# Bucketed attention and a squared-relu layer on one core: two stages instead of a mix, weight rounding spread out

## The chip, the cores and the metric

The kernel runs on one core of a Trainium2 chip. Its time is the device time of one execution in microseconds, the median of several runs. The profile is of one more execution. TensorE (PE, its weight loads PEld), VectorE (DVE), ScalarE (ACT) and GpSimd (POOL) run their own instruction streams in order and wait for each other by semaphores; SyncE (SP) only issues transfers here.

## What is computed

```python
# q, k, v: (4 batches, 8 heads, 768, 64) f32; proj: (64, 6); w_in: (512, 2048), w_out: (2048, 512), both float64
q_bucket = bits(q @ proj > 0);  k_bucket = bits(k @ proj > 0)
scores = where(q_bucket == k_bucket, q @ k.T / 8, -1e9)
attn = exp(scores - max);  attn = attn / (attn.sum(-1) + 1e-9)
x = (attn @ v), heads side by side        # (3072 tokens, 512)
out = maximum(x @ w_in, 0)**2 @ w_out     # (3072, 512)
```

## The kernel before

Attention works on 16 pairs of heads (`pr`), four pairs to a batch, and on 6 key tiles of 128 (`kt`) for each pair: 96 steps `u`. Keys lie on partitions, the 768 queries on columns in two halves of 384 (`HS`).

- `load_pair` (L206) brings q, k and v of a pair, on SP's queue, two pairs ahead.
- `features` (L223) transposes a half of q or k with three TensorE transposes; ScalarE copies the result out (`feat`). `hash_bits` (L237) multiplies it with the projections, and VectorE turns the sign into bits.
- `score` (L269) adds a bf16 product of bits, which drives keys of other buckets far down, and the f32 product of features. Two heads lie on the two halves of the rows. ScalarE's exponentials (L285) go to a ring of 8 tiles. The two score tiles take four of the eight PSUM banks, so a score begins only when the exponentials of the step before have read them.
- `add_up` (L293) adds the exponentials on VectorE, one step later; `attend` (L303) multiplies them with v into `xo`, two steps later. `xo` has one buffer.
- `sum_up` (L320) sums over partitions with a matrix of ones in two blocks of 64 columns, adds a small number by a bf16 matmul, and transposes (`flip`). `normalize` (L334) takes one reciprocal, transposes it back (`recs`) and multiplies it into `x_t` of the batch.
- A general path (`general`, L491) recomputes all if the values are large; `peak` (L250) collects the largest |q| and |k| for that decision, which is made at the very end (L469 to L484).

The weights arrive as float64 and are rounded by hand in 32 pieces of 128 x 512: `load_weight` (GpSimd's queue), `part_weight` (VectorE L120 and L124, GpSimd L129 and L132, ScalarE L135 `one`) and `round_weight` (VectorE L145 and L149, GpSimd L152).

The second part, `hidden` (L360) and `project` (L373), works on a half batch of 384 tokens: 16 groups of 4 matmuls with relu (ScalarE) and square (VectorE), then 3 groups of 16 matmuls for the output. An f32 matmul is two TensorE instructions ("passes" below), so the profile counts twice as many. A hidden or output group uses one of two PSUM banks (`bank`), which features, hashes and sums use too.

The order of every engine is written out by hand. A step u issues: loads of a later pair, `score(u)`, two pieces of weights (as long as there are any, so in the first 17 steps), two preparations for the next pair (features, hashes, peaks: they fill the first five steps of a pair), `add_up(u-1)`, `attend(u-2)`, after the last key tile the sums and the product, and then some of the waiting second part (`fill`, L400), which exists from the end of the first batch, step 25, on. The rest of the second part runs after the last step.

Of the kernel before, what the change touches and what calls it, by code (L numbers as in the profile page):

```python
# [23 lines left out]
TINY = 2.0**-100  # L24
# [9 lines left out]
def kernel(  # L34
# [28 lines left out]

    glob = ctx.enter_context(tc.tile_pool(name="glob", bufs=1))
# [8 lines left out]
    const = fast.enter_context(tc.tile_pool(name="const", bufs=1))  # L73
    p_qk = fast.enter_context(tc.tile_pool(name="p_qk", bufs=2))
    p_v = fast.enter_context(tc.tile_pool(name="p_v", bufs=3))
    p_f = fast.enter_context(tc.tile_pool(name="p_f", bufs=2))
    p_x = fast.enter_context(tc.tile_pool(name="p_x", bufs=2))
    p_n = fast.enter_context(tc.tile_pool(name="p_n", bufs=1))
    p_r = fast.enter_context(tc.tile_pool(name="p_r", bufs=2))
    ps_s = fast.enter_context(tc.tile_pool(name="ps_s", bufs=2, space=PSUM))  # L80
    ps_o = fast.enter_context(tc.tile_pool(name="ps_o", bufs=1, space=PSUM))
    ps_1 = fast.enter_context(tc.tile_pool(name="ps_1", bufs=2, space=PSUM))
# [17 lines left out]
    def load_weight(i, pool):  # L100
        src, r, c, dst = pieces[i]
        if src.dtype != U64:
            nc.gpsimd.dma_start(out=dst, in_=src[r:r + P, c:c + PIECE])
# [8 lines left out]
    def part_weight(i, pool):  # L112
# [4 lines left out]
        power = pool.tile([P, PIECE], U32, name="power")  # L117
        top = pool.tile([P, PIECE], U32, name="top")
        one = pool.tile([P, PIECE], FP32, name="one")
# [48 lines left out]
    ones = const.tile([P, D], FP32, name="ones")  # L168
    tinies = const.tile([P, D], BF16, name="tinies")
    units = const.tile([P, HS], BF16, name="units")  # L170
    peaks = const.tile([P, 2, NP], FP32, name="peaks")
# [3 lines left out]
    def constants():  # L175
        N = NBITS
        for h in range(2):
            r = h * D
            nc.scalar.dma_start(out=pj[r:r + D], in_=proj)
# [16 lines left out]
        nc.vector.memset(tinies, SB * TINY)  # L196
        nc.vector.memset(units, 1.0)
# [8 lines left out]
    def load_pair(pr):  # L206
        b, j = divmod(pr, PB)
        tiles = []
        for src, pool, name in ((q, p_qk, "q_nat"), (k, p_qk, "k_nat"), (v, p_v, "v_nat")):
            pair = src[b, 2 * j:2 * j + 2]  # L210
            if src is v:
                t = pool.tile([P, 2, SB * D], FP32, name=name)
                nc.sync.dma_start(out=t, in_=pair.rearrange("h (p t) d -> p h (t d)", t=SB))
            else:
                t = pool.tile([P, SB, 2, D], FP32, name=name)
                for h in range(2):
                    nc.sync.dma_start(
                        out=t[:, :, h], in_=pair[h].rearrange("(p t) d -> p t d", t=SB)
                    )
# [30 lines left out]
    def peak(pr, w):  # L250
        nc.vector.tensor_reduce(
            out=peaks[:, w, pr:pr + 1], in_=nat[pr][w].rearrange("p t h d -> p (t h d)"),
            axis=AXL.X, op=ALU.max, apply_absolute_value=True,
        )

    def prepare(pr):
        for w in range(2):
            for r in range(2):
                yield features, (pr, w, r)
        for w in range(2):  # L260
            for r in range(2):
                yield hash_bits, (pr, w, r)
        for w in range(2):
            yield peak, (pr, w)
# [26 lines left out]
    totals, outs = {}, {}  # L291
# [25 lines left out]
    x_t = {}  # L317
    flips = {}

    def sum_up(pr, c):  # L320

        tot = bank("tot")
        for h in range(2):
            rows = tot[h * D:(h + 1) * D, 0:HS]
            nc.tensor.matmul(  # L325
                out=rows, lhsT=ones, rhs=totals[pr, h][:, c * HS:(c + 1) * HS],
                start=True, stop=False,
            )
            nc.tensor.matmul(out=rows, lhsT=tinies, rhs=units, start=False, stop=True)  # L329
        if c == 0:  # L330
            flips[pr] = p_n.tile([P, S], FP32, name="flip")
        nc.vector.transpose(out=flips[pr][:, c * HS:(c + 1) * HS], in_=tot[:, 0:HS])  # L332

    def normalize(pr):  # L334

        b, j = divmod(pr, PB)
        if j == 0:
            x_t[b] = p_x.tile([P, NFT, S], FP32, name="x_t")
        rec = p_n.tile([P, S // 32], FP32, name="rec")
        nc.vector.reciprocal(  # L340
            out=rec, in_=flips[pr].rearrange("p (n f) -> p n f", f=32)[:, :, 0]
        )
        recs = p_n.tile([P, S], FP32, name="recs")
        nc.vector.transpose(
            out=recs.rearrange("p (n f) -> p n f", f=32),
            in_=rec.rearrange("p (n o) -> p n o", o=1).to_broadcast([P, S // 32, 32]),
        )
        xo = outs.pop(pr)
        for c in range(2):
            cut = slice(c * HS, (c + 1) * HS)  # L350
            nc.vector.scalar_tensor_tensor(  # L351
                out=x_t[b][:, j, cut], in0=xo[:, c, 0:HS], scalar=xo[:, 1, HS:HS + 1],
                in1=recs[:, cut], op0=ALU.add, op1=ALU.mult,
            )

    gates = {}

    def hidden(b, c, ff, pool):  # L360
        hp = bank("hid")
        for ft in range(NFT):
            nc.tensor.matmul(  # L363
                out=hp[:, 0:HS], lhsT=w_in[:, ft, ff * P:(ff + 1) * P],
                rhs=x_t[b][:, ft, c * HS:(c + 1) * HS], start=(ft == 0), stop=(ft == NFT - 1),
            )
        r = p_r.tile([P, HS], FP32, name="r")
        nc.scalar.activation(out=r, in_=hp[:, 0:HS], func=ACTF.Relu)  # L368
        g = pool.tile([P, HS], FP32, name="gate")
        nc.vector.tensor_tensor(out=g, in0=r, in1=r, op=ALU.mult)  # L370
        gates[b, c, ff] = g

    def project(b, t):  # L373
        c, i = divmod(t, SB // 2)
        y = bank("y")
        for ff in range(NFF):
            nc.tensor.matmul(  # L377
                out=y, lhsT=gates[b, c, ff][:, i * P:(i + 1) * P], rhs=w_out[:, ff],
                start=(ff == 0), stop=(ff == NFF - 1),
            )  # L380
        o = p_r.tile([P, DM], FP32, name="o")
        nc.scalar.copy(out=o, in_=y)  # L382
        nc.sync.dma_start(out=out_v[b, t], in_=o)

    def mlp(b, pool):
        for c in range(2):
            for ff in range(NFF):
                yield 2.7, hidden, (b, c, ff, pool)
            for i in range(SB // 2):
                yield 14.2, project, (b, c * (SB // 2) + i)  # L390

    steps = [(pr, kt) for pr in range(NP) for kt in range(SB)]
    SHARE = 7.2
    AHEAD = 2
    todo = []
    credit = [0.0]

    def fill(n):  # L400
        credit[0] += n
        while todo and credit[0] > 0:
            cost, f, args = todo.pop(0)
            f(*args)
            credit[0] -= cost
        if not todo:
            credit[0] = min(credit[0], 0.0)

    with tc.manual_schedule():
        load_pair(0)  # L410
        make_identity(nc, ident)
        constants()
        for pr in range(1, AHEAD):
            load_pair(pr)
        for f, args in prepare(0):
            f(*args)

        late = ExitStack()
        early = ExitStack()
        p_w = early.enter_context(tc.tile_pool(name="p_w", bufs=3))  # L420
        p_g = None
        LEAD = 3
        moved = 0
        for i in range(LEAD):
            load_weight(i, p_w)

        prep = []
        for u in range(len(steps) + 4):
            if u < len(steps):
                pr, kt = steps[u]  # L430
                if kt == 0:
                    if pr + AHEAD < NP:
                        load_pair(pr + AHEAD)
                    if pr + 1 < NP:
                        prep = list(prepare(pr + 1))
                score(pr, kt)
            for _ in range(2):
                if moved <= len(pieces):
                    if moved + LEAD < len(pieces):
                        load_weight(moved + LEAD, p_w)  # L440
                    if moved < len(pieces):
                        part_weight(moved, p_w)
                    if moved >= 1:
                        round_weight(moved - 1)
                    moved += 1
            if p_g is None and moved > len(pieces):
                early.close()
                p_g = late.enter_context(tc.tile_pool(name="p_g", bufs=NFF + 2))
            for _ in range(2):
                if prep:  # L450
                    f, args = prep.pop(0)
                    f(*args)
            if 1 <= u <= len(steps):
                add_up(*steps[u - 1])
            if 2 <= u <= len(steps) + 1:
                attend(*steps[u - 2])
            if u >= 2:
                pr, kt = steps[min(u - 2, len(steps) - 1)]
                if kt == SB - 1 and u - 2 < len(steps):
# [218 lines left out]
```

## Time and profile before

| what | value |
|---|---|
| median of 3 runs | 1202.77 us (1201.63 to 1202.92) |
| profiled execution: time, span | 1201.52 us, 1199.8 us |
| busy: PE, DVE, ACT, POOL | 1107.1, 440.3, 266.5, 113.0 us |
| mean granted TensorE clock | 0.962 of 2.4 GHz |
| HBM read, written | 35.65 MB, 6.29 MB |

The span is the time from the first to the last instruction of the profile; what lies outside it is the difference to the execution's time. Busy times are unions on an engine. The mean hides stages: the first 25 steps are attention alone with the weights beside it for 17 of them, then the second part of a finished batch is mixed into the steps of the next, and the last batch's second part stands alone at the end. Each of these is read by itself below.

### The profile page before, as it was taken

What the parts mean: (1) busy time and instruction counts of PE and PEld (TensorE: products, weight loads), DVE (VectorE), ACT (ScalarE), POOL (GpSimd) and SP (SyncE); (2) the same over time, 40 slices, a digit from 0 to 9 for tenths busy, and PEclk for the clock granted to TensorE, in tenths of its full rate; (3) what the DMA queues carried; (4) which work ended last, traced back from release to release, by engine and by line L of the source; (5) the groups of instructions that cost most, each with busy time, mean ns of one, the idle gap of its engine ahead of it and who ended that gap; (6) DMA issues with size and microseconds to landing.
All of it is one profiled execution on the core that took longest, in us unless ns stands there. A gap on an engine that the chain in (4) does not pass through costs nothing.

```text
span 1199.8 us, 10401 instructions
## 1 busy us (share of the span) xinstructions
PE 1107.1 (92%) x4226; PEld 529.5 (44%) x4226; DVE 440.3 (37%) x645; ACT 266.5 (22%) x441; POOL 113.0 (9%) x136
## 2 busy tenths in 40 slices
PE   4646369999999999999999999999999999999997
PEld 2222124455445544455445544455445544554543
DVE  3788889442224322342124322342124321310200
ACT  2222234322122211322122311322122211110110
POOL 2666661000000000000000000000000000000000
PEclk9767769999999999999999999999999999999999
DMA  7343321110010100110010100110000000000000
GB/s 205 106 114 119 114 101 40 41 27 14 17 36 14 27 22 10 49 27 14 18 36 14 27 22 10 49 27 14 18 9 1 1 9 9 9 1 17 9 9 20
DMA packets 62806, 42.68 MB, mean 36 GB/s; under 512 B 51488, under 2 KB 55584, under 8 KB 62752
## 3 DMA queue, kind: packets, MB, share of 16 engines
q1 hardware_dynamic: 57984, 25.17, 8.1%
q0 software_dynamic: 4608, 16.78, 4.2%
q8 instruction: 35, 0.57, 0.2%
q14 instruction: 19, 0.16, 0.0%
q10 hardware_dynamic: 160, 0.00, 0.0%
HBM read 35.65 MB, written 6.29 MB: 35 GB/s over the span
## 4 chain that ended last, share of the span: by engine, by line
PE 83%; DVE 9%; issue 3%; POOL 3%; DMA 1%; ACT 0%; SPq 0%; POOLq 0%; DVEq 0%; ACTq 0%
PE y L377 28%; PE hid L363 28%; PE st L278 12%; PE xo L310 10%; PE hp L242 3%; PE tp L230 2%; DVE one L149 2%; DVE total L299 2%; DVE power L145 2%; PE tot L325 2%; DVE power L120 1%; POOL power L129 1%; DMA q_nat<-in_q_dram 1%; POOL power L132 1%; POOL raw L106 1%
## 5 line engine op out<-in xcount | busy, mean ns | idle before, releaser
L363 PE MATMUL hid<-x_t,w_in 128*128 128x384 f32 x1024 | 342.1, 490 | 2.4 <-DVE x_t L351 2.4
L377 PE MATMUL y<-w_out,gate 128*128 128x512 f32 x768 | 334.4, 594 | 0.0
L363 PEld LDWEIGHTS hid<-x_t,w_in 128*128 128x128 f32 x1024 | 190.9, 190 | 152.1 <-ACT e L285 7.8
L377 PEld LDWEIGHTS y<-w_out,gate 128*128 128x128 f32 x768 | 144.7, 190 | 184.0 <-issue 175.3
L370 DVE TENSOR_TENSOR gate<-r 128x384 f32<-128x384 f32 x128 | 71.5, 558 | 329.6 <-ACT r L368 329.6
L285 ACT ACTIVATE e<-st 128x768 f32<-128x768 f32 x192 | 145.2, 809 | 140.2 <-PE st L278 136.5
L278 PE MATMUL st<-feat,feat 64*128 64x384 f32 x768 | 163.8, 499 | 0.0
L299 DVE TENSOR_TENSOR total<-total,e 128x768 f32<-128x768 f32 x128 | 118.2, 970 | 99.1 <-ACT e L285 99.1
L310 PE MATMUL xo<-e,v_nat 128*64 128x384 f32 (+1 forms) x768 | 152.5, 521 | 1.7 <-issue 1.6
L368 ACT ACTIVATE r<-hid 128x384 f32<-128x384 f32 x128 | 62.7, 490 | 328.1 <-PE hid L363 328.1
L278 PE MATMUL st<-bits,bits 64*128 64x384 bf16 x384 | 71.6, 336 | 27.0 <-ACT e L285 26.8
L382 ACT COPY o<-y 128x512 f32<-128x512 f32 x24 | 14.0, 585 | 341.7 <-PE y L377 244.7
L310 PEld LDWEIGHTS xo<-e,v_nat 128*64 128x64 f32 x768 | 48.6, 141 | 82.9 <-issue 79.3
L278 PEld LDWEIGHTS st<-feat,feat 64*128 64x128 f32 x768 | 72.0, 195 | 27.4 <-issue 26.5
L278 PEld LDWEIGHTS <-bits 64*128 64x128 bf16 x384 | 20.4, 94 | 96.5 <-issue 81.7
L332 DVE STREAM_TRANSPOSE flip<-tot 128x384 f32<-128x384 f32 x32 | 18.4, 579 | 103.3 <-PE tot L329 103.3
L145 DVE SCALAR_TENSOR_TENSOR power<-raw,power 128x512 uint32<-128x512 uint32 x32 | 44.5, 1390 | 27.7 <-POOL power L132 27.7
L245 DVE TENSOR_SCALAR bits<-hp,bar_k,gain_k 128x384 bf16<-128x384 f32 x32 | 21.0, 675 | 87.6 <-PE hp L242 87.6
L135 ACT ACTIVATE one<-top 128x512 f32<-128x512 uint32 x32 | 20.0, 630 | 104.3 <-DVE top L124 104.3
L245 DVE TENSOR_SCALAR bits<-hp,bar_q,gain_q 128x384 bf16<-128x384 f32 x32 | 20.7, 673 | 60.8 <-PE hp L242 60.8
L242 PE MATMUL hp<-feat,proj_k 128*128 128x384 f32 x64 | 29.0, 582 | 14.7 <-DVE bits L245 14.7
L325 PE MATMUL tot<-total,ones 128*64 128x384 f32 x128 | 28.6, 529 | 11.8 <-ACT feat L235 11.8
(55 smaller groups left out, 436.5 us busy)
## 6 DMA issues: line engine op xcount, KB each, us to landing
raw<-in_moe_w_in_dram POOLq DMA_DIRECT2D x16, 512.0 KB, 4.3
raw<-in_moe_w_out_dram POOLq DMA_DIRECT2D x16, 512.0 KB, 3.6
q_nat<-in_q_dram SPq DMA_DIRECT2D x32, 192.0 KB, 3.7
k_nat<-in_k_dram SPq DMA_DIRECT2D x32, 192.0 KB, 4.0
v_nat<-in_v_dram SPq DMA_DIRECT2D x16, 384.0 KB, 3.3
out_dram<-o SPq DMA_DIRECT2D x24, 256.0 KB, 2.0
pj<-in_proj_dram ACTq DMA_DIRECT2D x2, 1.5 KB, 2.3
```

Of the source, the lines that this page charges most:

```text
L145: nc.vector.scalar_tensor_tensor(out=power, in0=high, scalar=0x80000000, in1=power, op0=ALU.bitwise_and, op1=ALU.bitwise_or,)
L242: nc.tensor.matmul(out=hp[:, 0:HS], lhsT=projs[w], rhs=feat[pr, w][:, cut], start=True, stop=True)
L245: nc.vector.tensor_scalar(out=bits[pr, w][:, cut], in0=hp[:, 0:HS], scalar1=bars[w], scalar2=gains[w], op0=ALU.is_gt, op1=ALU.mult,)
L278: nc.tensor.matmul(out=st[h][:, c, 0:HS], lhsT=src[pr, 1][rows, key], rhs=src[pr, 0][rows, cut], start=first, stop=not first,)
L285: nc.scalar.activation(out=e[:, 0:S].rearrange("p (c f) -> p c f", c=2), in_=st[h][:, :, 0:HS], func=ACTF.Exp, scale=scale,)
L299: nc.vector.tensor_tensor(out=totals[pr, h], in0=in0, in1=weights[pr, kt, h][:, 0:S], op=ALU.add)
L310: nc.tensor.matmul(out=xo[h * D:(h + 1) * D, c, 0:n], lhsT=nat[pr][2][:, h, kt * D:(kt + 1) * D], rhs=weights[pr, kt, h][:, c * HS:c * HS ...
L325: nc.tensor.matmul(out=rows, lhsT=ones, rhs=totals[pr, h][:, c * HS:(c + 1) * HS], start=True, stop=False,)
L363: nc.tensor.matmul(out=hp[:, 0:HS], lhsT=w_in[:, ft, ff * P:(ff + 1) * P], rhs=x_t[b][:, ft, c * HS:(c + 1) * HS], start=(ft == 0), stop=( ...
L368: nc.scalar.activation(out=r, in_=hp[:, 0:HS], func=ACTF.Relu)
L370: nc.vector.tensor_tensor(out=g, in0=r, in1=r, op=ALU.mult)
L377: nc.tensor.matmul(out=y, lhsT=gates[b, c, ff][:, i * P:(i + 1) * P], rhs=w_out[:, ff], start=(ff == 0), stop=(ff == NFF - 1),)
```

## The change

- Two stages. The attention stage writes all of its output into one tile `x_t` of 4 x 3072 columns in SBUF; the second part follows in a stage of its own, with its own pools: 4 PSUM banks for hidden groups, 4 for outputs, 32 gate buffers.
- The second part works on 6 chunks of 512 tokens instead of 8 of 384.
- A piece of weights is loaded (on SP's queue, two raw buffers), parted and rounded in every third step, so all 96 steps have weights.
- `PREPARE` spreads the preparation of the next pair over all six steps.
- `sum_up` comes ahead of `attend` in its step. It sums in four column blocks of 32 (half and head), one f32 matmul each, and VectorE adds the small number (`once`), takes eight reciprocals of 32 partitions x 12, which also sort the blocks, and transposes back once.
- The largest |q| and |k| are collected in the second stage, from q and k loaded again in 16 pieces of 768 KB; the decision (`guard`) is made in chunk 3.
- The first k comes by ScalarE's queue, `proj` by GpSimd's.

```diff
-    p_x = fast.enter_context(tc.tile_pool(name="p_x", bufs=2))
+    x_t = fast.enter_context(tc.tile_pool(name="x_all", bufs=1)).tile([P, NFT, B * S], FP32, name="x_t")
+    p_w = first.enter_context(tc.tile_pool(name="p_w", bufs=2))
-        raw = pool.tile([P, PIECE, 2], U32, name="raw", bufs=4)
-        nc.gpsimd.dma_start(
+        raw = p_w.tile([P, PIECE, 2], U32, name="raw")
+        nc.sync.dma_start(
...
+        one = p_w.tile([P, PIECE], FP32, name="one")
+        top = one.bitcast(U32)
...
+    PREPARE = (
+        ((features, 0, 0), (features, 0, 1)),
+        ((features, 1, 0),),
+        ((features, 1, 1), (hash_bits, 0, 0)),
+        ((hash_bits, 0, 1),),
+        ((hash_bits, 1, 0),),
+        ((hash_bits, 1, 1),),
+    )
...
-    def sum_up(pr, c):
+    def sum_up(pr):
         tot = bank("tot")
-        for h in range(2):
-            rows = tot[h * D:(h + 1) * D, 0:HS]
-            nc.tensor.matmul(
-                out=rows, lhsT=ones, rhs=totals[pr, h][:, c * HS:(c + 1) * HS],
-                start=True, stop=False,
-            )
-            nc.tensor.matmul(out=rows, lhsT=tinies, rhs=units, start=False, stop=True)
+        for c in range(2):
+            for h in range(2):
+                g = 2 * h + c
+                nc.tensor.matmul(
+                    out=tot[g * 32:(g + 1) * 32, 0:HS], lhsT=ones,
+                    rhs=totals[pr, h][:, c * HS:(c + 1) * HS], start=True, stop=True,
+                )
+        flip = p_n.tile([P, HS], FP32, name="flip")
+        nc.vector.transpose(out=flip, in_=tot[:, 0:HS])
+        NB = HS // 32
+        once = p_n.tile([P, NB], FP32, name="once")
+        nc.vector.tensor_scalar(
+            out=once, in0=flip.rearrange("p (n f) -> p n f", f=32)[:, :, 0],
+            scalar1=S * TINY, scalar2=None, op0=ALU.add,
+        )
+        rec = p_n.tile([P, 2, NB], FP32, name="rec")
+        for g in range(4):
+            for c in range(2):
+                at = 64 * (g // 2) + 32 * c
+                nc.vector.reciprocal(
+                    out=rec[g * 32:(g + 1) * 32, c], in_=once[at:at + 32]
+                )
+        recs[pr] = p_n.tile([P, S], FP32, name="recs")
+        nc.vector.transpose(
+            out=recs[pr].rearrange("p (n f) -> p n f", f=32),
+            in_=rec.rearrange("p c (n o) -> p (c n) o", o=1).to_broadcast([P, S // 32, 32]),
+        )
...
+        for u in range(len(steps) + 2):
+            if u < len(steps):
+                pr, kt = steps[u]
+                if kt == 0 and pr + AHEAD < NP:
+                    load_pair(pr + AHEAD, nc.sync)
                 score(pr, kt)
+            done = steps[u - 2] if u >= 2 else None
+            if done is not None:
+                if done[1] == SB - 1:
+                    sum_up(done[0])
+                attend(*done)
+                if done[1] == SB - 1:
+                    normalize(done[0])
+            if u < len(steps) and pr + 1 < NP:
+                for f, w, r in PREPARE[kt]:
+                    f(pr + 1, w, r)
             if 1 <= u <= len(steps):
                 add_up(*steps[u - 1])
+            i, r = divmod(u, EVERY)
+            if r == 0:
+                if i < len(pieces):
+                    load_weight(i)
+                if 0 <= i - 1 < len(pieces):
+                    part_weight(i - 1)
+            if r == 1 and 0 <= i - 1 < len(pieces):
+                round_weight(i - 1)
...
+        for i in range(NCHUNK):
+            gates = []
+            for ff in range(NFF):
+                hp = ps_h.tile([P, NCH], FP32, name="hid")
+                for ft in range(NFT):
+                    nc.tensor.matmul(
+                        out=hp, lhsT=w_in[:, ft, ff * P:(ff + 1) * P],
+                        rhs=x_t[:, ft, i * NCH:(i + 1) * NCH],
+                        start=(ft == 0), stop=(ft == NFT - 1),
+                    )
+                r = p_r.tile([P, NCH], FP32, name="r")
+                nc.scalar.activation(out=r, in_=hp, func=ACTF.Relu)
+                g = p_g.tile([P, NCH], FP32, name="gate")
+                nc.vector.tensor_tensor(out=g, in0=r, in1=r, op=ALU.mult)
+                gates.append(g)
+                if i in (1, 2) and ff % 2 == 0:
+                    peak(i - 1, ff // 2)
+                if i == 3 and ff == 8:
+                    guard()
+            for n in range(NCH // P):
+                y = ps_y.tile([P, DM], FP32, name="y")
+                for ff in range(NFF):
+                    nc.tensor.matmul(
+                        out=y, lhsT=gates[ff][:, n * P:(n + 1) * P], rhs=w_out[:, ff],
+                        start=(ff == 0), stop=(ff == NFF - 1),
+                    )
+                o = p_r.tile([P, DM], FP32, name="o")
+                nc.scalar.copy(out=o, in_=y)
+                b, t = divmod(i * (NCH // P) + n, SB)
+                nc.sync.dma_start(out=out_v[b, t], in_=o)
```

## Rows read from the trace of the kernel before

**Rows 1.** Stretches of 20 us: each engine's busy us (instructions), granted clock, DMA share, GB/s.
```profile
140.00:160.00 20.00, 8.14 (x26) 3.63 (x25) 17.07 (x20) 5.69 (x10) 13.56 (x17) 0.50 0.35 125
200.00:220.00 20.00, 20.00 (x119) 8.86 (x117) 13.51 (x18) 8.22 (x13) 0.00 (x0) 1.00 0.18 40
```

**Rows 2.** Timeline at 74 us: start, duration, engine, line, operation, [idle before <-releaser].
```profile
74.52 0.63 ACT L135 ACTIVATE one<-top 128x512 f32<-128x512 uint32 x1 [1.25 <-DVE top L124]
...
75.05 1.49 ACT L285 ACTIVATE e<-st 128x768 f32<-128x768 f32 x2
...
75.89 0.48 PE L278 MATMUL st<-bits,bits 64*128 64x384 bf16 x1 [5.39 <-ACT e L285]
```

**Rows 3.** Timeline of TensorE, 197 to 226 us: a pair without weights.
```profile
197.39 0.34 PE L278 MATMUL st<-bits,bits 64*128 64x384 bf16 x2
...
206.77 0.34 PE L278 MATMUL st<-bits,bits 64*128 64x384 bf16 x2
...
208.49 1.51 PE L310 MATMUL xo<-e,v_nat 128*64 128x384 f32 x8
...
209.93 0.55 PE L278 MATMUL st<-bits,bits 64*128 64x384 bf16 x2
...
219.21 0.87 PE L230 MATMUL tp<-ident,k_nat 128*128 128x128 f32 x6
220.01 1.51 PE L310 MATMUL xo<-e,v_nat 128*64 128x384 f32 x8
221.35 0.81 PE L325 MATMUL tot<-total,ones 128*64 128x384 f32 x4
...
223.12 2.17 PE L363 MATMUL hid<-x_t,w_in 128*128 128x384 f32 x6
225.93 6.04 PE L363 MATMUL hid<-x_t,w_in 128*128 128x384 f32 x18 [0.64 <-DVE x_t L351]
```

**Rows 4.** The chain that ended last, in order of time: start, us, what.
```profile
203.90 1.49 PE hp L242 x4
...
1069.00 41.20 PE y L377 x96
1110.20 41.28 PE hid L363 x128
```

**Rows 5.** Timeline of VectorE, 197 to 208 us.
```profile
197.50 0.58 DVE L332 STREAM_TRANSPOSE flip<-tot 128x384 f32<-128x384 f32 x1 [0.22 <-PE tot L329]
198.12 0.30 DVE L340 RECIPROCAL rec<-flip 128x24 f32<-128x24 f32 x1
198.45 0.98 DVE L344 STREAM_TRANSPOSE recs<-rec 128x768 f32<-128x768 f32 x1
199.47 1.15 DVE L351 SCALAR_TENSOR_TENSOR x_t<-xo,recs 128x384 f32<-128x384 f32 x2
...
204.79 1.32 DVE L245 TENSOR_SCALAR bits<-hp,bar_k,gain_k 128x384 bf16<-128x384 f32 x2 [1.27 <-PE hp L242]
206.03 1.82 DVE L299 TENSOR_TENSOR total<-total,e 128x768 f32<-128x768 f32 x2
```

**Rows 6.** Timeline of VectorE: small copies at the start, and `top` twice.
```profile
2.77 0.24 DVE L192 COPY proj_q<-pj 64x6 f32<-64x6 f32 x2 [1.53 <-DMA pj<-in_proj_dram]
...
22.05 0.42 DVE L124 TENSOR_SCALAR top<-raw 128x512 uint32<-128x512 uint32 x1
...
180.76 1.48 DVE L124 TENSOR_SCALAR top<-raw 128x512 uint32<-128x512 uint32 x1
```

**Rows 7.** Timeline of TensorE at the start.
```profile
12.50 1.51 PE L230 MATMUL tp<-ident,q_nat 128*128 128x128 f32 x6 [12.50 <-DMA q_nat<-in_q_dram]
...
19.49 0.34 PE L278 MATMUL st<-bits,bits 64*128 64x384 bf16 x2
```

**Rows 8.** DMA issues: queue, count, KB each, median us from issue to landing.
```profile
q_nat<-in_q_dram SPq DMA_DIRECT2D x32, 192.0 KB, 3.7
```

**Rows 9.** Timeline at the end.
```profile
1193.04 0.58 ACT L382 COPY o<-y 128x512 f32<-128x512 f32 x1 [13.47 <-PE tp L477]
```

More of the change, by code (lines that the diff above doesn't have):

```diff
@@ L289, in score @@
             weights[pr, kt, h] = e
-    totals, outs = {}, {}
+    totals, outs, recs = {}, {}, {}
     def add_up(pr, kt):
@@ L334, in normalize @@
     def normalize(pr):
         b, j = divmod(pr, PB)
[L337 to L347, printed above, removed]
@@ L351, in normalize @@
             nc.vector.scalar_tensor_tensor(
-                out=x_t[b][:, j, cut], in0=xo[:, c, 0:HS], scalar=xo[:, 1, HS:HS + 1],
-                in1=recs[:, cut], op0=ALU.add, op1=ALU.mult,
-            )
[L358 to L390, printed above, removed]
+                out=x_t[:, j, b * S + c * HS:b * S + (c + 1) * HS],
+                in0=xo[:, c, 0:HS], scalar=xo[:, 1, HS:HS + 1],
+                in1=recs[pr][:, cut], op0=ALU.add, op1=ALU.mult,
+            )
     steps = [(pr, kt) for pr in range(NP) for kt in range(SB)]
-    SHARE = 7.2
     AHEAD = 2
[L397 to L407, printed above, removed]
+    EVERY = 3
     with tc.manual_schedule():
-        load_pair(0)
+        load_pair(0, nc.scalar)
         make_identity(nc, ident)
@@ L413 @@
         for pr in range(1, AHEAD):
[L414 to L428, printed above, removed]
+            load_pair(pr, nc.sync)
+        for w in range(2):
+            for r in range(2):
+                features(0, w, r)
+            for r in range(2):
+                hash_bits(0, w, r)
@@ L453 @@
+            if u < len(steps) and pr + 1 < NP:
+                for f, w, r in PREPARE[kt]:
+                    f(pr + 1, w, r)
             if 1 <= u <= len(steps):
                 add_up(*steps[u - 1])
[L455 to L459, printed above, removed]
-                    for c in range(2):
-                        sum_up(pr, c)
-                    normalize(pr)
-                    if pr % PB == PB - 1:
-                        todo.extend(mlp(pr // PB, p_g))
@@ L465 @@
-            fill(SHARE)
-        fill(1e9)
-        top = p_n.tile([P, 2], FP32, name="top2")
-        for w in range(2):
+            i, r = divmod(u, EVERY)
[6 more added lines that the diff above has]
+                round_weight(i - 1)
+        for i in sorted(raws):
+            if i not in parts:
+                part_weight(i)
+            round_weight(i)
@@ L471, with peak @@
+        def peak(w, i):
+            n = B * H * S * D // P // NPK
+            t = p_k.tile([P, n], FP32, name="raw_qk")
+            flat = (q, k)[w].rearrange("b h s d -> (b h s d)").rearrange("(p f) -> p f", p=P)
+            nc.sync.dma_start(out=t, in_=flat[:, i * n:(i + 1) * n])
             nc.vector.tensor_reduce(
[L472 to L477 removed]
```

127 lines of the change are left out of this document (50 added, 77 removed).

## The prediction

> **What bounds the kernel now.** I read the table of stretches first, then the timeline of a slow stretch, then that of a clean one. In the stretch from 140 us, TensorE is busy 8.14 of 20 us at a granted clock of 0.50, that is 1.2 GHz of its 2.4, while VectorE is busy 17 and GpSimd 13.6. From 200 us TensorE is busy all 20 us at clock 1.00 and GpSimd does nothing [rows 1]. The weight rounding separates the two stretches. The timeline at 74 us shows how: ScalarE's `one` (L135) waits for VectorE's `top`, the exponentials (L285) stand behind `one` in ScalarE's order, and the next score matmul (L278) has waited 5.39 us for them [rows 2]. Two pieces of weights in each step are more than VectorE and this chain carry.
>
> The loss can be counted. The score of step 0 starts at 19.49 [rows 7], that of step 20 (the first after the sums of pair 2) at 197.39 [rows 3]: 8.9 us a step. The six steps that follow, without weights and without second part, take from 197.39 to 223.12, so 25.73 us a pair or 4.29 a step [rows 3]. Twenty steps at 4.29 are 86 us, not 178: 92 us are lost to the rounding. After that TensorE has no idle time worth naming, so the rest of the kernel is the sum of its matmuls.
>
> **A pair without weights, as TensorE's slots** [rows 3, 4]. A score takes 206.77 to 208.49 = 1.72 us, an attend 208.49 to 209.93 = 1.44, the six transposes of two features 219.21 to 220.01 = 0.80 (0.40 a feature), four hash matmuls 1.49 (0.75 for one call), the sums of a pair 221.35 to 223.12 = 1.77. A pair is then 6 x (1.72 + 1.44) + 4 x 0.40 + 4 x 0.745 + 1.77 = 25.31. Measured are 25.73; the 0.42 between is the wait for the exponentials in the two steps that have no preparation (in one of them the first two bit matmuls span 0.55 instead of 0.34, so 0.21 each). The slots are therefore good for the new stage.
>
> **The change, part by part.**
> Sums in four column blocks: the before-order runs two blocks at a time, 4 passes in sequence plus two bf16 additions, 1.77. The new order has one 2-pass matmul in each of four blocks and no additions. Bounds: 0.65 if all four run beside each other (two passes), 1.45 if only two do. I take 0.80, since the pairs of blocks do run together in the rows. A pair of the new stage has a floor of 24.34.
>
> Preparation spread over all six steps (PREPARE) gives each step at least 0.40 of extra TensorE work between attend and next score; this covers the 0.21 of the exponentials. `peak` leaves VectorE.
>
> Where waits come from in the new order. I lay one pair out by hand, each engine in program order.
>
> (a) The totals. In step kt=1 (score, sums, attend, one feature) the sums end 2.52 us after its start, and the next pair's first attend is wanted after the following score, at 1.72 + 0.80 + 1.44 + 0.40 + 1.72 = 6.08. It needs xo (one buffer), which `normalize` frees. VectorE does: flip 0.58, `once` about 0.20, eight reciprocals, recs 0.98, two products 1.15, each about 0.04 after the one before [rows 5]. No row shows a reciprocal of 32 partitions x 12. The row of 128 x 24 has 0.30, and small independent copies follow each other so closely that two take 0.24 [rows 5, 6]. The bounds are therefore eight times 0.08 and eight times 0.30; I take 0.20 each, 1.6. The chain ends at 2.52 + 0.62 + 0.24 + 1.64 + 1.02 + 1.15 = 7.19: TensorE waits 1.1 us (0.15 at the low price, 1.9 at the high one).
>
> The Trainium skill has a rule on this, in "VectorE: DVE Perf Modes", section "Two Vector instructions with no wait between them": an instruction whose input or output begins in another group of 32 partitions than that of the instruction before is held until all earlier Vector instructions have finished. The eight reciprocals change their input group at every one, so by it none would overlap; at the high price that would be 13 us more in the whole kernel, and 15 us less if they overlapped as the copies do. No row of this case shows two such instructions behind each other.
>
> (b) The weights. One piece in three steps: `part_weight` in kt=0 and kt=3, `round_weight` in kt=1 and kt=4. In kt=3 VectorE first waits for the hash matmul, which is last in TensorE's step: hash starts at 1.72 + 1.44 = 3.16, its result is there 0.89 later (203.90 to 204.79), so 4.05; bits 0.66, two additions 1.82, `power` and `top` 0.76 (0.42, overlapping by 0.08) [rows 4 to 6] end at 7.3; ScalarE's `one` takes 0.63 [rows 2], to 7.9. Behind it stand the exponentials of kt=4, which would have been ready at 3.91 + 1.72 = 5.6; they run 1.49, to 9.4. The score of kt=5 could start at 7.82 but needs both score tiles back: it ends near 9.4 + 1.7 = 11.1 instead of 9.54. TensorE waits 1.6 us. If `top` is stretched by GpSimd's work as in the row of 1.48, this is 2.6; if VectorE comes earlier than I think, 0. In kt=0 there is no hash before the additions, `one` ends at about 6.0 and the exponentials it delays are wanted only at 8.3: no cost. `round_weight` in kt=1 stands behind the products and delays nothing that TensorE needs; in kt=4 it ends before the next bits.
>
> (c) Queues. The 32 weight loads leave GpSimd's queue for SP's, behind the loads of pair pr+2, and each waits for one of two raw buffers. What is queued behind them are the loads of the next pairs, issued a whole pair (27 us) before their first use against 3.7 us to land [rows 8]. I cost it at nothing; without that cover it would be a few us a pair. GpSimd keeps three operations a piece and no DMA.
>
> A pair: 24.34 + 1.1 + 1.6 = 27.0; 16 pairs are 432. The first pair has no earlier attends, sums and wait in its first two steps (-4.8), which are then bound by score plus exponentials, 3.2 each (+1.8). The last has no preparation (-4.6) and no wait (b) (-1.6) but six waits of 0.21 (+1.3). The last two attends and sums come behind (+3.7). Together -4.2.
>
> Start: transposes at 12.50 and score at 19.49 now [rows 7], with four weight loads in flight beside q. In the new order no weights move then and k comes by another queue. q at its median landing alone would be there near 5, as now at 12.5; I take 7.3, for q and k together at the present rate, and the same 7.0 us to the score: 14.3.
>
> Second part: 96 passes of y take 41.20 us, 0.429 for 512 columns; 128 of 384 columns take 41.28 [rows 4]. The new hidden passes are 768 of 512 instead of 1024 of 384: 1536 x 0.4292 = 659.2, half a microsecond less than now. No gap stands in these rows with two PSUM buffers, so four bring nothing. The 16 new loads of q and k and their maxima lie beside: a maximum of 1536 columns is priced like two additions, 1.82 [rows 5], one for two hidden groups of 3.4 us each. Without that cover they would cost up to 29 us. Between the stages: a hidden group that reads the tile being written ran six passes before it waited 0.64 for the last quarter [rows 3], so waits go by region, and chunk 0 reads only batch 0. I take 0, with 0 to 5 us for pools that are handed over.
>
> End: the last copy of y starts at 1193.04 of 1199.8 [rows 9]: 6.8 us, kept.
>
> **Sum.** 14.3 + 432 - 4.2 + 659.2 + 6.8 = 1108.1 of span, beside 1199.8. The profiled execution took 1201.5, so 1.7 lies around its span: 1109.8. The median of the runs is 1202.8, another 1.2 more: 1111.
>
> **The rivals.** *No waits in the stage*: VectorE comes early, reciprocals are cheap, a pair costs its floor. 1111 - 16 x 2.7 + 1.6 = 1069. For it: the clean pair hid everything but 0.42. Against: the two chains above. *Longer waits*: high prices of (a) and (b), a pair of 28.9, 1141; with one more microsecond a pair for something the timetable misses, 1157. For it: the row of 1.48, where GpSimd and VectorE met. *The clock falls, and the change loses*: the attention stage loses the matmuls that the second part put between its steps; if its waits cost the clock, slots double (0.50 in the stretch from 140 us). A pair would be up to 48.7 + 2.7 = 51.4, the kernel 1501; it is slower than before once a pair costs 27.0 + 92/16 = 32.7, that is once about a quarter of the stage runs at 1.2 GHz. Against it: attention alone keeps clock 1.00 from 200 us, and the waits that I expect are under 2 us, where the low clock came with waits of 5 and more [rows 1, 2]. *The change does not spread the load*: the rounding still stops the exponentials and the 92 us come back elsewhere, about 1200; against it, one piece in three steps is a sixth of the present rate.
>
> **How the numbers follow.** Forecast 0.5, no waits 0.22, longer waits 0.23, clock 0.03, no gain 0.02. The range reaches to both nearer rivals: 1062 to 1152. The measurement tells 0.2% from no change; by these cases faster 0.95, same 0.01, slower 0.04.
>
> **What would show it.** The score of step 0 near 14 us; then pairs of 27 us with one wait of about 1 us of xo for the products, behind kt=1, and one of 1.6 us of the score for the exponentials, behind kt=3; eight reciprocals of about 0.2; second part from about 442 us without a gap, 0.429 a pass; clock 1.00 all through. A pair outside 24.3 to 29.5, or a clock under 0.95 in the stage, would make the prediction wrong.

## The result, and the profile after

The changed kernel takes 1124.16 us (median of 4 runs, 1123.84 to 1124.46) against 1202.55, a ratio of 0.9349 [0.9333, 0.9365]: 78.4 us less. The forecast was 1111, in a range of 1062 to 1152, so the way and the size are right and the time is 13 us longer than the sum. The kernel times here are medians; one execution of the last version below (`orders_kt3_six`) took 2227.53 us, while the other three of that version took 1077.35 to 1077.99, and as no trace of it was kept its cause is open.

The page of the profile after, first busy times and then the 40 slices of the span:

```profile
span 1122.1 us, 9897 instructions
PE 1067.4 (95%) x3906; PEld 466.6 (42%) x3906; DVE 418.7 (37%) x707; ACT 265.2 (24%) x409; POOL 88.6 (8%) x106
PE   6999999999999998999999999999999999999998
DVE  2777777777777778520034103400120012001100
POOL 0111111111111112100000000000000000000000
PEclk9999999999999999999999999999999999999999
```

GpSimd's work lies evenly over the first 16 slices, and TensorE never falls to the 8 of 20 us of [rows 1]. The granted clock is 0.998 of 2.4 GHz over the whole. A stretch of the attention stage, beside the hand-over to the second part (columns as in [rows 1]):

```profile
200.00:300.00 100.00, 89.90 (x535) 38.54 (x534) 72.97 (x131) 45.09 (x68) 18.60 (x22) 1.00 0.28 76
440.00:460.00 20.00, 20.00 (x99) 7.99 (x96) 19.40 (x31) 6.39 (x9) 6.53 (x6) 0.96 0.08 27
```

From 200 to 300 us TensorE is busy for 90 of 100 us at a clock of 1.00. Of the ten idle ones 8.9 stand in what the prediction called waits (a) and (b), 4.4 and 4.5. TensorE's waits over the whole span by the line that ended them, in total, times, longest:

```profile
PE xo L306 <- issue: 22.6, 15, 2.0
PE st L274 <- ACT e L281: 18.0, 33, 0.8
```

One pair in the timeline of TensorE (score L274, attend L306, feature L232, hash L244, sums L320), to be compared with [rows 3]:

```profile
183.08 0.85 PE L320 MATMUL tot<-total,ones 128*32 128x384 f32 x8
...
185.79 0.34 PE L274 MATMUL st<-bits,bits 64*128 64x384 bf16 x2
...
189.05 1.51 PE L306 MATMUL xo<-e,v_nat 128*64 128x384 f32 x8 [1.48 <-issue]
...
190.50 0.55 PE L232 MATMUL tp<-ident,k_nat 128*128 128x128 f32 x3
190.88 0.81 PE L244 MATMUL hp<-feat,proj_q 128*128 128x384 f32 x2
191.62 0.34 PE L274 MATMUL st<-bits,bits 64*128 64x384 bf16 x2
...
194.78 0.91 PE L244 MATMUL hp<-feat,proj_q 128*128 128x384 f32 x2
195.63 0.34 PE L274 MATMUL st<-bits,bits 64*128 64x384 bf16 x2
...
198.79 0.91 PE L244 MATMUL hp<-feat,proj_k 128*128 128x384 f32 x2
200.45 0.32 PE L274 MATMUL st<-bits,bits 64*128 64x384 bf16 x1 [0.74 <-ACT e L281]
201.15 0.32 PE L274 MATMUL st<-bits,bits 64*128 64x384 bf16 x1 [0.38 <-ACT e L281]
...
202.85 1.51 PE L306 MATMUL xo<-e,v_nat 128*64 128x384 f32 x8
...
213.53 0.34 PE L274 MATMUL st<-bits,bits 64*128 64x384 bf16 x2
```

From the score of kt=2 at 185.79 to the next one at 213.53 a pair is 27.74 us (forecast 27.0). Both waits stand where the timetable had them: 1.48 us before the attend that opens a pair, and the score of kt=5, which could start at 199.64 behind the hash and ends at 202.85, 3.21 us instead of 1.72. Behind the first wait stands VectorE's chain after the sums:

```profile
211.75 0.58 DVE L325 STREAM_TRANSPOSE flip<-tot 128x384 f32<-128x384 f32 x1 [1.68 <-PE tot L320]
212.36 0.17 DVE L328 TENSOR_SCALAR once<-flip 128x12 f32<-128x12 f32 x1
212.57 1.84 DVE L336 RECIPROCAL rec<-once 32x12 f32<-32x12 f32 x8
214.45 0.98 DVE L340 STREAM_TRANSPOSE recs<-rec 128x768 f32<-128x768 f32 x1
215.54 1.15 DVE L350 SCALAR_TENSOR_TENSOR x_t<-xo,recs 128x384 f32<-128x384 f32 x2
```

The products end at 216.69, and the attend starts at 216.79: the profile calls this wait "issue", but it ends 0.10 us after the products (the test is `prep_first`, below). Behind the second stands ScalarE:

```profile
199.07 0.63 ACT L142 ACTIVATE one<-one 128x512 f32<-128x512 uint32 x1 [4.05 <-DVE one L131]
199.60 1.49 ACT L281 ACTIVATE e<-st 128x768 f32<-128x768 f32 x2
```

ScalarE stood idle for 4.05 us in front of `one`, with the exponentials queued behind it. It is the picture of [rows 2] at a smaller price.

### The profile page after: what moved, and what is told of

The parts are those of the page before. It is cut to its first block, busy times and chain, and to the rows that moved or that the text cites. A ratio compares the mean times of both kernels' runs of the same rounds, so it can differ in the third digit from the quotient of the medians.

```text
span 1122.1 us, 9897 instructions
## 1 busy us (share of the span) xinstructions
PE 1067.4 (95%) x3906; PEld 466.6 (42%) x3906; DVE 418.7 (37%) x707; ACT 265.2 (24%) x409; POOL 88.6 (8%) x106
## 3 DMA queue, kind: packets, MB, share of 16 engines
q1 hardware_dynamic: 63328, 54.14, 16.7%
## 4 chain that ended last, share of the span: by engine, by line
PE 89%; DVE 4%; issue 4%; ACT 2%; DMA 0%; SPq 0%; ACTq 0%; DVEq 0%
PE hid L453 29%; PE y L470 29%; PE st L274 13%; PE xo L306 11%; PE hp L244 3%; DVE total L295 2%; PE tp L232 2%; ACT e L281 2%; PE tot L320 1%; DVE power L127 1%; DVE one L131 1%; DMA q_nat<-in_q_dram 0%; DVE bits L247 0%; DVE gate L461 0%; SPq L219 0%
## 5 line engine op out<-in xcount | busy, mean ns | idle before, releaser
L453 PE MATMUL hid<-x_t,w_in 128*128 128x512 f32 x768 | 330.8, 592 | 0.0
L461 DVE TENSOR_TENSOR gate<-r 128x512 f32<-128x512 f32 x96 | 66.5, 693 | 506.3 <-ACT r L459 504.9
L453 PEld LDWEIGHTS hid<-x_t,w_in 128*128 128x128 f32 x768 | 145.8, 190 | 183.4 <-issue 182.7
L306 PE MATMUL xo<-e,v_nat 128*64 128x384 f32 (+1 forms) x768 | 146.2, 502 | 22.6 <-issue 22.6
L274 PE MATMUL st<-feat,feat 64*128 64x384 f32 x768 | 158.5, 486 | 0.0
L459 ACT ACTIVATE r<-hid 128x512 f32<-128x512 f32 x96 | 57.3, 597 | 275.9 <-PE hid L453 275.9
L306 PEld LDWEIGHTS xo<-e,v_nat 128*64 128x64 f32 x768 | 48.2, 136 | 110.5 <-issue 107.9
L274 PE MATMUL st<-bits,bits 64*128 64x384 bf16 x384 | 70.6, 327 | 18.2 <-ACT e L281 18.0
L274 PEld LDWEIGHTS st<-feat,feat 64*128 64x128 f32 x768 | 69.6, 189 | 31.5 <-issue 31.4
L274 PEld LDWEIGHTS <-bits 64*128 64x128 bf16 x384 | 21.0, 93 | 65.2 <-issue 52.8
L237 ACT COPY feat<-tp 128x384 f32<-128x384 f32 x64 | 29.2, 481 | 55.6 <-PE tp L232 55.6
L136 POOL TENSOR_SCALAR power<-power 128x512 uint32<-128x512 uint32 x32 | 23.9, 748 | 211.0 <-DVE power L127 211.0
L142 ACT ACTIVATE one<-one 128x512 f32<-128x512 uint32 x32 | 20.1, 629 | 70.8 <-DVE one L131 70.7
L295 DVE TENSOR_TENSOR total<-e,e 128x768 f32<-128x768 f32 x32 | 30.2, 984 | 0.0
L244 PE MATMUL hp<-feat,proj_k 128*128 128x384 f32 x64 | 28.9, 536 | 0.0
```

The source lines that it names most:

```text
L136: nc.gpsimd.tensor_scalar(out=power, in0=power, scalar1=1151.0, scalar2=896.0, op0=ALU.min, op1=ALU.max,)
L237: nc.scalar.copy(out=feat[pr, w][:, r * HS:(r + 1) * HS], in_=tp[:, 0:HS])
L244: nc.tensor.matmul(out=hp[:, 0:HS], lhsT=projs[w], rhs=feat[pr, w][:, cut], start=True, stop=True)
L274: nc.tensor.matmul(out=st[h][:, c, 0:HS], lhsT=src[pr, 1][rows, key], rhs=src[pr, 0][rows, cut], start=first, stop=not first,)
L295: nc.vector.tensor_tensor(out=totals[pr, h], in0=in0, in1=weights[pr, kt, h][:, 0:S], op=ALU.add)
L306: nc.tensor.matmul(out=xo[h * D:(h + 1) * D, c, 0:n], lhsT=nat[pr][2][:, h, kt * D:(kt + 1) * D], rhs=weights[pr, kt, h][:, c * HS:c * HS ...
```

## Experiments

All are changes of the changed kernel (1124.16 us) unless another is named. Each was timed beside the kernel before, whose median in these comparisons lay between 1201.5 and 1202.1.

### The pace of the weights

```diff
-            i, r = divmod(u, EVERY)
...
+            for _ in range(2):
+                if moved <= len(pieces):
+                    if moved + LEAD < len(pieces):
+                        load_weight(moved + LEAD)
+                    if moved < len(pieces):
+                        part_weight(moved)
+                    if moved >= 1:
+                        round_weight(moved - 1)
+                    moved += 1
```

> The change with the weights at the pace of the kernel before: two pieces in each of the first 17 steps (four raw buffers, six exponential tiles so that they fit). Theory: the gain comes from the spreading; 17 steps at 8.9 us instead of 4.6 cost 73 us, and the other 13 pairs lose their wait of 1.4 behind one: 1124.2 + 73 - 18 = about 1180. Rival: the gain comes from the two stages, the larger chunks and the sums: the pace matters little, below 1140.

1187.9 us, ratio 0.9879 [0.9863, 0.9896]: 63.7 us of the 78.4 go with the old pace (the smaller ring, the raw buffers and the three loads ahead, which this pace needs, were not tried by themselves). The table of stretches shows the old picture in the new order:

```profile
60.00:100.00 40.00, 25.62 (x100) 10.70 (x97) 34.16 (x52) 12.12 (x20) 22.86 (x24) 0.74 0.44 130
```

TensorE is busy 25.6 of 40 us at a clock of 0.74, VectorE 34 and GpSimd 23. Where the 63.7 us arise, and what is left of the gain, is read from the scores of step 0, of step 20 and of the same step one pair later:

```profile
14.22 0.34 PE L274 MATMUL st<-bits,bits 64*128 64x384 bf16 x2
...
186.34 0.34 PE L274 MATMUL st<-bits,bits 64*128 64x384 bf16 x2
...
212.63 0.34 PE L274 MATMUL st<-bits,bits 64*128 64x384 bf16 x2
```

The first 20 steps take 172.1 us, where the changed kernel takes 88.3 (14.22 to 102.53): 83.8 more. The pairs behind them have no weights and take 26.29 us instead of 27.74, which gives back 19 in 13 pairs; by the two profiled spans 65.0 are left.

Against the kernel before, this run is 12.7 us shorter by the two profiled spans. Of these, 5.3 are the start (14.22 against 19.49 [rows 7]), 5.8 the first 20 steps (172.1 against 177.9) and 1.6 the end, from the last copy of y on. From step 20 to that copy both kernels take 995.7 us (186.34 to 1182.03, and 197.39 to 1193.04 [rows 3, 9]). So the two stages, with the new sums and the new preparation in them, gain nothing there by themselves.

The same from the other side, in the kernel before:

```diff
-            for _ in range(2):
+            for _ in range(2 if u % 3 == 0 else 1):
                 if moved <= len(pieces):
```

> The kernel before with four pieces of weights in three steps instead of six, the slowest pace at which they are ready when its mixed second part begins at step 25. Theory: VectorE, at up to 3.3 us a piece beside GpSimd, is still the bound: 25 steps of about 6.9 us against 17 of 8.9 and 8 of 4.3, so 13 us less than 1202.6, about 1190; the mixed order leaves no room to spread. Rival: the pace alone is enough, and most of the 92 us come back without two stages: 1140 or less.

1192.96 us, ratio 0.9926 [0.9909, 0.9943]: 9 us, near the theory's 13. As long as the second part starts with the first batch, the weights must be ready by step 25, and at that pace VectorE is still busy for 33.6 of the 40 us from 60 us on. What the two stages bring is 96 steps for the weights. A pace between these two, with a later start of the second part, was not tried.

### The size of the chunks

```diff
-    NCH = 512
+    NCH = 384
```

> The change with chunks of 384 tokens in the second part, eight of them. Theory: passes of 384 columns cost 0.3225 and those of 512 cost 0.430, the same for each column, and nothing waits: 1124 to 1127. Rival: the larger chunks or the four PSUM banks carry part of the gain: 10 us or more are lost.

1123.76 us, ratio 0.935 [0.9334, 0.9365], as with 512. The larger chunks carry none of the gain (the four PSUM banks stayed; they were not tried alone). The trace has 331.8 us in 1024 hidden passes, against 330.8 in 768.

### The wait for xo

```diff
+                if done[1] == 0 and pr + 1 < NP:
+                    for f, w, r in PREPARE[kt]:
+                        f(pr + 1, w, r)
                 attend(*done)
...
-            if u < len(steps) and pr + 1 < NP:
+            if u < len(steps) and pr + 1 < NP and not (done is not None and done[1] == 0):
```

> In the step whose attend opens a new pair, the preparation (one feature, one hash) comes ahead of the attend; nothing else changes. Theory: TensorE waits 1.48 us there for xo, which VectorE's eight reciprocals and the products free late; 0.40 + 0.85 us of preparation in front of it leave 0.25. 15 times 1.2 us: 1124.2 becomes about 1106. Rival: the 1.48 us, which the profile calls issue, are TensorE's own (another array layout, weight loads): they move with the attend, and the time stays at 1124.

1107.47 us, ratio 0.9213 [0.9197, 0.9228]: 16.7 us less. What is left of the wait now has its right name:

```profile
PE xo L306 <- DVE x_t L350: 4.3, 14, 0.3
```

14 times 0.3 us instead of 14 times 1.5; the fifteenth wait, of 2.0 us in the last pair, which has no preparation to put in front, stays. The rival of TensorE's own time falls.

```diff
-        tot = bank("tot")
+        flip = p_n.tile([P, S], FP32, name="flip")
         for c in range(2):
+            tot = bank("tot")
             for h in range(2):
-                g = 2 * h + c
+                rows = tot[h * D:(h + 1) * D, 0:HS]
...
+                nc.tensor.matmul(out=rows, lhsT=tinies, rhs=units, start=False, stop=True)
+            nc.vector.transpose(out=flip[:, c * HS:(c + 1) * HS], in_=tot[:, 0:HS])
+        rec = p_n.tile([P, S // 32], FP32, name="rec")
+        nc.vector.reciprocal(
+            out=rec, in_=flip.rearrange("p (n f) -> p n f", f=32)[:, :, 0]
+        )
```

> The change without its four-block sums: two blocks of 64 columns, the bf16 additions, two transposes and one reciprocal as in the kernel before, still ahead of the attend. Theory: TensorE pays 0.97 us a pair more, but VectorE's chain of 4.7 us behind the sums shrinks to about 3.1 and the wait of 1.48 for xo goes: 1124.2 + 15.5 - 22 = 1117, faster than with the four blocks. Rival: the four blocks save what they take off TensorE, and their loss costs 15 us: 1140.

1113.46 us, ratio 0.9265 [0.9249, 0.928]: without the four blocks the kernel is 10.7 us faster than with them. The sums take TensorE from 206.52 to the attend at 208.19, 1.67 us instead of 0.78 (183.08 to the attend at 183.86 in the changed kernel). VectorE's chain behind them is shorter:

```profile
208.41 0.58 DVE L328 STREAM_TRANSPOSE flip<-tot 128x384 f32<-128x384 f32 x1 [0.23 <-PE tot L327]
209.03 0.30 DVE L330 RECIPROCAL rec<-flip 128x24 f32<-128x24 f32 x1
209.37 0.98 DVE L334 STREAM_TRANSPOSE recs<-rec 128x768 f32<-128x768 f32 x1
```

One reciprocal of 0.30 stands where eight took 1.84, and of the 22.6 us of waits for xo one of 0.3 us is left. The four blocks, as the change has them, save 0.9 us a pair on TensorE and cost 1.5 in a wait; without them a pair takes 27.03 us instead of 27.74.

```diff
-                nc.vector.reciprocal(
-                    out=rec[g * 32:(g + 1) * 32, c], in_=once[at:at + 32]
-                )
+                nc.vector.reciprocal(out=rec[:, 2 * g + c], in_=once)
```

> The change with the eight reciprocals each taken over all 128 partitions x 12, so that all begin in the same group of 32 partitions; their blocks are not sorted and 1.0 is added to the totals, so the denominators are others. Theory (by the rule on starting groups): each still takes 0.22, but they follow each other at about 0.12, the chain is 0.85 shorter and so is the wait for xo: 1111. Rival: eight reciprocals take 8 x 0.23 wherever they begin: 1124.

1105.9 us, ratio 0.9202 [0.9187, 0.9217]: 18 us less.

```profile
205.50 0.83 DVE L335 RECIPROCAL rec<-once 128x12 f32<-128x12 f32 x8
206.25 0.92 DVE L337 STREAM_TRANSPOSE recs<-rec 128x768 f32<-128x768 f32 x1
```

Eight reciprocals that begin in the same group of partitions take 0.83 us, 0.10 apart, although one of them spans 0.177 on average, so they overlap; with changing groups they take 1.84, 0.23 apart, which is a little more than one of them spans (0.219). By the rule in the Trainium skill, "VectorE: DVE Perf Modes", section "Two Vector instructions with no wait between them", the second kind is held and the first is not; the two traces agree with it. Each reciprocal here also covers four times the partitions, so it is not a smaller amount of work that makes them quicker; eight of 32 partitions with one start were not run, but the copies of [rows 6], on 64 partitions and with one start, overlap too. The gain is larger than expected because the chain from `flip` to the end of the products is 1.18 us shorter (3.76 instead of 4.94), not 0.85: the reciprocals give 1.01, and the transposition behind them, which reads only the first two of them here, starts 0.08 us before the last one ends and takes 0.92 us instead of 0.98.

### The wait behind `one`

```diff
+            i, r3 = divmod(u, EVERY)
+            if r3 == 0 and 0 <= i - 1 < len(pieces):
+                part_weight(i - 1)
             done = steps[u - 2] if u >= 2 else None
...
-                if 0 <= i - 1 < len(pieces):
-                    part_weight(i - 1)
```

> VectorE's two operations of part_weight, and ScalarE's one behind them, are issued ahead of the step's hash and additions instead of behind them. Theory: the wait of the score in kt=5 (0.74 + 0.38 us and a stretched score, 1.4 in all) comes from the exponentials that stand behind one; they go, 15 times 1.4 us: about 1103. Rival: the wait is the exponentials' own pace, with one set of score tiles: it stays, 1120 to 1124.

1113.44 us, ratio 0.926 [0.9244, 0.9275]: 10.7 us less, half of what was expected, though the wait for the exponentials is gone from the list (18.0 us before, now 1.1). The timeline of step kt=0, where the piece now stands ahead of the last additions, shows what came instead:

```profile
201.87 2.65 DVE L295 TENSOR_TENSOR total<-total,e 128x768 f32<-128x768 f32 x2
...
202.51 1.21 POOL L139 TENSOR_SCALAR power<-power 128x512 uint32<-128x512 uint32 x1
...
203.98 1.45 PE L320 MATMUL tot<-total,ones 128*32 128x384 f32 x8
```

The additions start later and last 2.65 us instead of 1.82, beside GpSimd's work; they end at 204.52, and the sums, which begin at 203.98, span 1.45 instead of 0.85. So 0.6 us of the 1.5 that a pair wins are lost again: it takes 26.82 us instead of 27.74. The list of waits counts only 3.8 us in all for the totals, for the group had begun. Hence only kt=3 should be moved:

```diff
+            early = u % SB == 3
+            if r3 == 0 and early and 0 <= i - 1 < len(pieces):
+                part_weight(i - 1)
...
+                if not early and 0 <= i - 1 < len(pieces):
+                    part_weight(i - 1)
```

> part_weight ahead of hash and additions in kt=3 only; in kt=0 it stays behind the additions as in the change. Theory: moving it in kt=0 put GpSimd's work beside the last additions (2.65 us instead of 1.82), made the totals late and stretched the sums from 0.85 to 1.45 us; without that the whole of the wait behind one comes back, 15 times 1.4: about 1103. Rival: the shortfall of part_early (10.7 us instead of 21) has another cause, and this stays near 1113.

1101.11 us, ratio 0.9163 [0.9148, 0.9179]: 23 us less, a pair of 26.25 us, and the sums are back at 0.85:

```profile
200.31 0.85 PE L320 MATMUL tot<-total,ones 128*32 128x384 f32 x8
```

### Both together

> Both of these orders together. Theory: two independent waits, so the gains add: 1124.2 - 18 - 21 = 1085, a pair of about 25.1 us. Rival: with one wait gone VectorE is late elsewhere, and the sum is not reached: 1095 to 1103.

1096.52 us, ratio 0.9123 [0.9108, 0.9138]. This run stood ahead of the one with kt=3 alone. Its two gains add (16.7 + 10.7 = 27.4; measured 27.6), so the two waits are independent; the number fell short because one of the gains did.

> As part_early_kt3, with the preparation ahead of the attend that opens a pair. Theory: the gains add, 1124.2 - 16.7 - 21 = about 1086. Rival: 1096, as both_orders.

1085.12 us, ratio 0.9029 [0.9012, 0.9046]: 39.0 us less than the changed kernel, against 16.7 + 23.1 = 39.8.

```diff
+        for c in range(2):
+            nc.vector.reciprocal(out=rec[:, c], in_=once)
         for g in range(4):
-            for c in range(2):
-                at = 64 * (g // 2) + 32 * c
-                nc.vector.reciprocal(
-                    out=rec[g * 32:(g + 1) * 32, c], in_=once[at:at + 32]
-                )
+            c = 1 - g % 2
+            at = 64 * (g // 2) + 32 * c
+            nc.vector.reciprocal(
+                out=rec[g * 32:(g + 1) * 32, c], in_=once[at:at + 32]
+            )
```

> As orders_kt3, with six reciprocals instead of eight: two over all 128 partitions, which get the blocks that need no move, and four of 32 partitions for the others. Theory: two follow each other at 0.10, four stand alone at 0.23, so 1.1 us instead of 1.84, more than the 0.3 us a pair that TensorE still waits for xo: 4 us less than orders_kt3, about 1082. Rival: the writes over one another cost what is saved: no change.

1077.81 us, ratio 0.8965 [0.8947, 0.8983], the lowest median of all versions: 46 us less than the changed kernel, and 7 less than without this edit, where 4 were expected.

```profile
217.53 0.31 DVE L334 RECIPROCAL rec<-once 128x12 f32<-128x12 f32 x2
217.88 0.92 DVE L338 RECIPROCAL rec<-once 32x12 f32<-32x12 f32 x4
```

The chain has shrunk by 0.6 us, and the wait of 14 times 0.3 us for xo no longer stands among TensorE's waits: a pair takes 24.70 us instead of 25.08. That is 5 us in 14 pairs. The others come from the last pair, where TensorE's wait for xo goes from 1.78 to 1.20 us and that for the totals from 1.85 to 0.18.

## Why the prediction was right, and where it was off

**What bounds the kernel before.** Right. It gave 92 us of the first 20 steps to the rounding's pace; with that pace the first 20 steps of the new order are 83.8 us longer. Restoring the pace costs less in the whole, 63.7, because the pairs without weights are then free of wait (b), which is the price of the spreading (`part_early_kt3`: 23 us). How much of the 83.8 us is VectorE's load, how much the exponentials behind `one`, and how much the lower clock was not tried apart.

**Start.** Forecast 14.3, measured 14.22. That it is so close is luck: q was there at 6.9 (forecast 7.3), and from there to the score it took 7.3 (forecast 7.0). `two_per_step` issues three loads of weights ahead of step 0 and starts at 14.22 too, so the absence of weights is not what gave the time; that leaves the new queues of k, `proj` and the weights, which were not tried apart.

```profile
6.93 1.51 PE L232 MATMUL tp<-ident,q_nat 128*128 128x128 f32 x6 [6.93 <-DMA q_nat<-in_q_dram]
...
14.22 0.34 PE L274 MATMUL st<-bits,bits 64*128 64x384 bf16 x2
```

**The pair.** Right in mechanism, 0.74 us too low in size, which is 12 us in 16 pairs and nearly the whole miss. Three terms:
- Wait (a) is 1.48 us, not 1.1. The reciprocals were put at 0.20 between bounds of 0.08 and 0.30 and cost 0.23, 0.24 us more in all. The rule on starting groups that the prediction takes from the Trainium skill ("VectorE: DVE Perf Modes", section "Two Vector instructions with no wait between them") says that none of them overlaps, and none does; the measured price of a single one is below the 0.30 that the row of 24 columns gave. Most of the rest are two hand-overs that the sum had at nothing: `flip` begins 0.14 us behind the sums (211.61 to 211.75), and the attend 0.10 us behind the products.
- The preparation costs 4.96 us a pair, not 4.58. The sum took 0.40 for a feature and 0.745 for a hash from rows where two of them follow each other ([rows 3, 4]). In the new order three of the four hashes stand alone between an attend and a score and take 0.85 each (194.78 to 195.63), and one feature alone takes 0.48 (185.31 to 185.79); the feature and hash that stand together take 1.12 (190.50 to 191.62). These terms were taken as known and were not: a slot out of a group of two was used for one standing alone.
- Wait (b) is 1.49, not 1.6. Its places, kt=3 with a price and kt=0 without one, were as forecast; part_early_kt3 shows it.

**The sums.** The four blocks do run beside each other: they take 0.78 us, against the 0.80 that was taken. That their own chain takes back more than they save was in the prediction as wait (a), but it was not held against the saving, a step that the prediction left out: 0.97 less a pair on TensorE and 1.1 more in a wait is no gain, by the prediction's own numbers, since nothing else in the new order delayed xo.

**Queues, clock, second part.** The loads on SP's queue delayed nothing that TensorE needs; among its waits only that for the first q ends with a DMA. The rival of a falling clock came in one place only. From 200 to 300 us the waits of each pair, the longest 1.5 us, went with a granted clock of 1.00. In the last pair TensorE waited 1.96 us for xo, and behind that wait the clock stood at 0.50, that is at 1.2 GHz, and then at 1.00 again:

```profile
438.22 2.72 PE L306 MATMUL xo<-e,v_nat 128*64 128x384 f32 x8 [1.96 <-issue]
```

```profile
438.50:441.50 3.00, 3.00 (x12) 1.24 (x10) 3.00 (x4) 0.00 (x0) 1.91 (x1) 0.50 0.39 126
445.00:450.00 5.00, 5.00 (x33) 2.29 (x32) 5.00 (x6) 1.99 (x4) 2.65 (x3) 1.00 0.00 0
```

The attend took 2.72 us there instead of 1.51. The prediction's ground against this rival, that the low clock had come with waits of 5 us and more, does not hold; the price stayed small because it happened once.

The stage began its second part at 455.49 (forecast 442.1) and its last copy at 1116.99, so the second part took 661.5 us, not 659.2. Of the 13.4 us by which it began late, 12 are the pairs; the rest lies in the first and the last pair, where the slow attend alone is 1.2. Of the second part's excess two microseconds are the decision, whose two transposes stand in TensorE's order and wait for VectorE:

```profile
PE tp L436 <- DVE top L430: 1.6, 1, 1.6
```

The prediction had the maxima beside the matmuls, which is right (16 of 1.75 us, no wait by TensorE for them), and left out the transposes. The end took 5.1 us instead of 6.8. So the span is 455.5 + 661.5 + 5.1 = 1122.1 against 442.1 + 659.2 + 6.8 = 1108.1.

**The rivals.** *No waits* is wrong for the change but is nearly what the last version reaches: 1077.8 against its 1069, a pair of 24.70 us against the floor of 24.34. *Longer waits* (1141) and *the change does not spread the load* (1200) are out. That an order of the same work could fill most of the waits (1085.1 us by order alone) was not seen: the timetable that found the two waits also says what could be put into them.

## What to carry to other kernels

Where an engine's queue is in order, look for the side work that stands ahead of the main work and waits itself: here two pieces of weights a step cost 84 us in the new order, with VectorE's load, the exponentials held up and the lower clock together; at one piece in three steps the one small ScalarE operation in front of the exponentials still cost 23, and these came back once it stood earlier in the right step. A timetable of one period, made from the profile's own durations, found both waits to 0.4 us; take the duration of a call from rows where it stands in the same company. Then use the timetable once more, to see which independent work could fill the waits. A saving on the engine that sets the pace must be weighed against the chain that it hangs on the others.

## What the runs showed of the hardware

- Reciprocals on VectorE whose input begins in another group of 32 partitions than that of the one before did not overlap: eight of 32 partitions x 12 took 1.84 us. Eight of 128 x 12 that all begin in one group overlapped and took 0.83.
- Beside GpSimd's work, two f32 additions on VectorE with both inputs in SBUF took 2.65 us instead of 1.82, and GpSimd's second operation on `power` 1.21 instead of 0.62 (`part_early`).
- A call whose operand shapes differ from its neighbours' (128*128 between the attend's 128*64 and the score's 64*128) cost more alone than in company: a hash of two passes 0.85 us and a feature 0.48, a feature and a hash together 1.12. That the change of shape is the reason was not tested.
- TensorE's granted clock fell to 0.50 once in the changed kernel, for a few microseconds behind a wait of 1.96 us, and stayed at 1.00 from 200 to 300 us beside waits of up to 1.5.
- The profile can call a wait "issue" that ends with another engine's work: 22.6 us before the attend, of which `prep_first` left 4.3 under the products' name and 2.0 under "issue".
